# Loading one of six operands in runs of four tokens: a chunked delta-rule attention with a spectral mixer behind it

## The chip, the cores and the metric

The kernel runs on one core of one Trainium2 chip. The metric is the device time of one execution in microseconds (us), where lower is better. Five executions of the kernel before took 219.13 to 220.66 us, with a median of 219.2 us.

## The reference, cut to what matters

Two stages stand behind each other. The first is a recurrence over 768 tokens for each of 4 x 8 = 32 heads with a 40 x 40 state; the second mixes tokens and channels.

```
for t in range(768):                       # state: [B, H, 40, 40]
    y[t]  = r[t] @ state
    Sa    = state @ a[t]
    state = state * w[t] - outer(Sa, b[t]) + outer(v[t], k[t])
x = y as [B, 768, 320]                     # heads side by side
theta = x @ w_theta
y = w_tok_r @ (x * cos(theta)) + w_tok_i @ (x * sin(theta))    # over tokens
u = x + y
out = u + relu(u @ w_ch)
```

All six inputs r, k, v, w, a, b lie in memory as [batch 4, head 8, token 768, 40] in float32. One token of one head is therefore a run of 160 bytes, and the tokens of one head follow each other without a gap.

## The kernel before, in words

The 768 tokens of a batch are cut into 6 chunks of 128, so there are 24 **tiles** (`i` = 0 to 23), each with 128 tokens on the partitions and 8 heads x 40 on the free axis.

`load(i)` gives six transfers a tile, one for each operand (`raw_w`, `raw_kb` twice, `raw_a`, `raw_rv` twice), each read as `"h t d -> t h d"`: 1024 runs of 160 bytes. They are issued from SP's queue (line L414), into four buffers for each operand.

`prep(i)` takes the logarithm of w on ScalarE (ACT) (`ln`, L423), sums it over tokens with triangular matrices on TensorE (PE) (`cs`, L430 to L440), and exponentiates the sums (`exp`, L445) into `ex`, where the two halves hold the inverse and the plain decay. k, b (`kb`, L452) and a (`ah`, L456) are multiplied by them on GpSimd (POOL); r and v are only cast to bf16 on POOL (`rv`, L461). For the first two tiles this is on VectorE (DVE) and ACT instead. Then `transpose_pairs` (L396) turns each bf16 operand on PE, two heads at a time (heads 2g and 2g+1, each padded from 40 to 64, make one 128-wide block), and ACT copies the result out of PSUM (L399), read as 32-bit words: `kbT`, `rvT` (both 1024 bf16 columns, or 512 words) and `aT` (512 columns, or 256 words).

`attention_scores(i)` and `readout(i)` multiply such transposed blocks with each other (L484, two heads side by side in the PE array) and DVE masks the result (L489): `psi`, `phi`, `lamv`, `lamu`, one DVE pass of 128 x 1024 each. `recurrence(i)` carries the state from chunk to chunk (`x0`, `nx`, `nu`, `gt`, `gd`), and the readout gives `x` (L624), which is transposed and multiplied by `w_theta` (L631, first use).

Of each batch, when all six chunks are done, ACT takes sines and cosines (L655), POOL multiplies them with x (`zr`, `zi`, L667), and `mix_row` runs 12 matmuls of 320 columns for each of six output rows (L685), then the residual (L695), a transpose (L588), the channel product (L631), the ReLU and sum (L704) and the store (SP, L707). The token weights for this are fetched once, in six pairs of transfers issued from POOL (`wtok_block`, L725: 128 x 768 of `w_tok_r` and of `w_tok_i`), and transposed on PE (L733). `mixer_weights` fetches `w_theta` and `w_ch` from POOL (L713, L716).

The order of the work is not that of the source. Every step is an `Op` with an assumed cost, the tiles it reads and writes, and a priority from the tables `TIMES` (a due time for each tile, each mixer row and each weight transfer) and `OFF` (an offset for each kind of step). `Plan.order` makes one list from these before anything is issued, and each engine's instructions stand in the order of that list. PSUM has eight banks: four are used as two double banks (`ps_d`, for the scores and `cs`), four as single banks (`ps_s`, for everything else).

Of the kernel before, what the change touches and what calls it, by code (L numbers as in the profile page):

```python
# [9 lines left out]
FP32 = mybir.dt.float32  # L10
# [216 lines left out]
def tail(n):  # L227
# [4 lines left out]
    ah=-29.76, ch=42.32, cs=-23.68, ea=-5.68, egd=-64.18, egt=9.05, ekb=-1.05, enu=-33.25,  # L232
    enut=-26.71, erv=-11.79, eth=-30.49, eut=-42.87, ewt=25.44, ex=-7.68, exp=-112.65,
    ext=9.87, gd=25.41, gt=10.89, kb=6.58, ln=-1.17, load=-12.1, mlu=70.45, mlv=15.71,
    mphi=35.75, mpsi=75.19, nu=-16.23, nut=3.78, nx=-57.27, oo=43, row=42.66, rv=9.85,
    sin=53.93, slu=-3.56, slv=6.28, sphi=-11.65, spsi=-15.12, st=42.29, ta=1.92, th=30.73,
    tkb=-0.04, trv=-1.76, uadd=20.68, ut=30.15, wdma=56, wt=28.14, x0=-37.84, xt=23.63,
    y=-16.87, z=-2.05)
WAIT, TSWITCH = 416.01, 546374.0
TIMES = dict(  # L240
    tile=[
        -39.53, -34.24, -29.51, -3.78, 20.04, 41.89, 38.94, 51.03, 56.49, 58.19, 71.7, 90.01,
        94.38, 97.37, 114.43, 121.89, 126.37, 125.37, 126.65, 137.15, 152.75, 154.06, 155.36,
        173.39],
    row=[
        51.82, 57.24, 68.97, 70.44, 94.9, 101.27, 93.77, 118.11, 124.13, 107.33, 127.65,
        140.22, 116.14, 132.99, 161.62, 121.8, 167.43, 194.51, 178.51, 189.99, 186.39, 240.98,
        241.1, 195.27],
    rel=[
        -29.38, 28.51, 59.76, 33.74, 24.97, 97.39, 29.98, 104.9])  # L250
# [3 lines left out]
def kernel(  # L254
# [35 lines left out]
    raw_rv = sb("raw_rv", [128, 2, H, D], FP32, 4)  # L290

    def load(i):
        bi, ci = divmod(i, NCH)

        def src(ap):
            return ap[bi, :, ci * C:(ci + 1) * C, :].rearrange("h t d -> t h d")
        s = i % 4
        return ((("raw_w", s), raw_w[s], src(w)),
                (("raw_k", s), raw_kb[s][:, 0], src(k)),
                (("raw_b", s), raw_kb[s][:, 1], src(b)),  # L300
                (("raw_a", s), raw_a[s], src(a)),
                (("raw_r", s), raw_rv[s][:, 0], src(r)),
                (("raw_v", s), raw_rv[s][:, 1], src(v)))
# [34 lines left out]
    rv_t = padded("rv", [128, 2, H, 64], NRV, last24)  # L338
# [12 lines left out]
    ex_t = sb("ex", [128, 2, 328], FP32, NEX)  # L351
    aT_t = sb("aT", [128, 512], BF16, NTR)
    kbT_t = sb("kbT", [128, 1024], BF16, NTR)
    rvT_t = sb("rvT", [128, 1024], BF16, NTR + 1)
# [57 lines left out]
    def loads(i):  # L412
        for key, dst, src in load(i):
            add("SP", "load", i, lambda dst=dst, src=src: nc.sync.dma_start(out=dst, in_=src),  # L414
                650, [], [key], work=1030)

    def prep(i):
# [3 lines left out]
        kb, rv, ah = kb_t[i % NKB], rv_t[i % NRV], ah_t[i % 3]  # L421
        kex = ("ex", i % NEX)
        add("ACT", "ln", i, lambda: nc.scalar.activation(  # L423
            out=lw[:, :, 0:D], in_=raw_w[s4], func=AF.Ln), 473,
# [3 lines left out]
        def cs():  # L428
            t = ps(pk)
            nc.tensor.matmul(t[:, 0, 0:DM], lhsT=ntri_inc, rhs=lw[:, :, 0:D],  # L430
# [6 lines left out]
            for g in range(G):  # L437
                nc.tensor.matmul(t[:, 1, DM + 2 * g:DM + 2 * g + 2], lhsT=pair(lw, g),
                                 rhs=ones2, start=False, stop=True, skip_group_check=True)
            nc.tensor.matmul(t[:, 0, DM:DM + 8], lhsT=ident,  # L440
                             rhs=off_diag.rearrange("p g c -> p (g c)"),
                             start=True, stop=True, skip_group_check=True)
        add("PE", "cs", i, cs, 2 * mm(320) + 6 * 25, [("lw", s2)], [pk], new=(pk, 2),
            tail=tail(8))
        add("ACT", "exp", i, lambda: nc.scalar.activation(  # L445
            out=ex, in_=ps(pk)[:, :, 0:328], func=AF.Exp), 717, [pk], [kex], table="lnexp")
        invW = ex[:, 0, 0:DM].rearrange("p (h d) -> p h d", h=H)
        Wi = ex[:, 1, 0:DM].rearrange("p (h d) -> p h d", h=H)
        fast = i < 2
        for j, nm in enumerate("kb"):  # L450
            add("DVE" if fast else "POOL", "kb", i,
                lambda j=j: (nc.vector if fast else nc.gpsimd).tensor_tensor(  # L452
                    out=kb[:, j, :, 0:D], in0=raw_kb[s4][:, j], in1=invW, op=ALU.mult),
                490 if fast else 864, [("raw_" + nm, s4), kex], [("kb", j, i % NKB)])
        add("DVE" if fast else "POOL", "ah", i,
            lambda: (nc.vector if fast else nc.gpsimd).tensor_tensor(  # L456
                out=ah[:, :, 0:D], in0=raw_a[s4], in1=Wi, op=ALU.mult),
            490 if fast else 864, [("raw_a", s4), kex], [("ah", i % 3)])
        for j, nm in enumerate("rv"):
            add("ACT" if fast else "POOL", "rv", i,  # L460
                lambda j=j: (nc.scalar.copy if fast else nc.gpsimd.tensor_copy)(  # L461
                    out=rv[:, j, :, 0:D], in_=raw_rv[s4][:, j]),
                460, [("raw_" + nm, s4)], [("rv", j, i % NRV)])

        def tr(kind, kinde, srcs, dst, skeys, dkey, eng):
# [8 lines left out]
        tr("trv", "erv", (rv[:, 0], rv[:, 1]), rvT_t[i % (NTR + 1)],  # L474
           [("rv", 0, i % NRV), ("rv", 1, i % NRV)], ("rvT", i % (NTR + 1)), "ACT")
# [18 lines left out]
    def attention_scores(i):  # L494
        st, s2 = i % NTR, i % NSC
        kbT, aT, rvT = kbT_t[st], aT_t[st], rvT_t[i % (NTR + 1)]
# [4 lines left out]
        scores(i, "slv", "mlv", rvT[:, 512:], rvT[:, 0:512], [("rvT", i % (NTR + 1))],  # L501
               lamv_t[s2], ("lamv", s2), mask_p)

    def recurrence(i):
        first, last = i % NCH == 0, i % NCH == NCH - 1
        st, s2 = i % NTR, i % 2
        aT, kb, rv = aT_t[st], kb_t[i % NKB], rv_t[i % NRV]
# [3 lines left out]
        vb = rv[:, 1]  # L511
        pk = ("ps", "x0", i)

        def x0():
# [13 lines left out]
            [("aT", st), ("psi", i % NSC), ("rv", 1, i % NRV)] +  # L528
# [14 lines left out]
        if not last:  # L543
            gk = ("ps", "gt", i)

            def gt_mm():
# [12 lines left out]
                [("kb", 0, i % NKB), ("kb", 1, i % NKB), ("rv", 1, i % NRV), ("nu", s2)] +  # L559
# [254 lines left out]
```

## Time and profile before

| | |
|---|---|
| median of five runs | 219.2 us |
| the profiled execution's own time | 219.2 us |
| its span, first to last instruction | 217.3 us |
| TensorE clock granted | 0.999 |
| PE busy | 196.8 us (91%), 3368 matmuls |
| DVE busy | 165.9 us (76%) |
| ACT busy | 146.7 us (68%) |
| POOL busy | 118.4 us (54%) |
| loads and stores of SP's queue (q1) | 153216 packets, 27.54 MB, 70.1% of the 16 DMA engines' span |
| weights of POOL's queue (q0) | 2432 packets, 2.77 MB, 7.7% |

An engine's busy time is the union of its instructions' times, and matmuls that overlap in the array count once, so a PE that is busy all the time need not be at its peak. "Packets" are the pieces that the DMA engines move, one for each contiguous run. The page also cuts the span into 40 equal slices and gives the busy share of each in tenths.

### The profile page before, as it was taken

To read this page: it belongs to the slowest core of one execution; us is meant where nothing else is said; L and a number is where in the kernel's file an instruction comes from. 1 tells how busy PE (TensorE), PEld (TensorE's weight loads), DVE (VectorE), ACT (ScalarE), POOL (GpSimd) and SP (SyncE) were. 2 spreads that over 40 slices of the span, in tenths; PEclk is the share of its full clock that TensorE was granted. 3 is DMA by queue.
4 is the path that set the end of the run, shared out by engine and by line. 5 is a ranking of instruction groups with operands and counts; after the bars stand their busy time and mean duration, and the time that the engine had idled before them with its cause. 6 is when DMAs were issued, how large, how long until landed. Compare 5 with 4: busy or idle time off the path is not lost.

```text
span 217.3 us, 8118 instructions
## 1 busy us (share of the span) xinstructions
PE 196.8 (91%) x3368; PEld 155.5 (72%) x3368; DVE 165.9 (76%) x250; ACT 146.7 (68%) x319; POOL 118.4 (54%) x184
## 2 busy tenths in 40 slices
PE   1497898879897899999999999999999999999993
PEld 1375766657677688687787778878787888777771
DVE  7468678875989758888999668888979978866533
ACT  3356675978679769978459946899599764863111
POOL 5000688297673992894762972697658660165000
PEclk9999999999999999999999999999999999999999
DMA  6998999999999999999988999898897010101122
GB/s 112 195 186 152 168 154 161 177 178 160 159 184 165 172 182 160 181 199 182 170 151 160 150 188 156 179 182 153 151 209 128 33 63 5 60 33 60 33 91 91
DMA packets 155684, 30.81 MB, mean 142 GB/s; under 512 B 150400, under 2 KB 155648, under 8 KB 155648
## 3 DMA queue, kind: packets, MB, share of 16 engines
q1 hardware_dynamic: 153216, 27.54, 70.1%
q0 software_dynamic: 2432, 2.77, 7.7%
q8 instruction: 26, 0.43, 0.8%
q14 instruction: 10, 0.08, 0.1%
HBM read 29.13 MB, written 3.93 MB: 152 GB/s over the span
## 4 chain that ended last, share of the span: by engine, by line
PE 72%; DVE 9%; ACT 5%; DMA 5%; POOL 3%; issue 3%; SPq 1%; ACTq 0%; DVEq 0%; POOLq 0%
PE ps_s L685 19%; PE ps_s L396 14%; PE ps_d L484 10%; PE ps_s L631 8%; PE ps_s L588 4%; DVE lamu L489 3%; DMA wrow_i<-in_moe_w_tok_i_dram 3%; DMA raw_a<-in_a_dram 2%; PE ps_s L617 2%; PE ps_s L536 2%; DVE psi L489 2%; PE ps_s L524 2%; PE ps_s L554 2%; PE ps_s L615 2%; DVE phi L489 2%
## 5 line engine op out<-in xcount | busy, mean ns | idle before, releaser
L452 POOL TENSOR_TENSOR kb<-raw_kb,ex 128x320 bf16<-128x320 f32 x44 | 37.4, 862 | 18.1 <-ACT ex L445 16.5
L685 PE MATMUL ps_s<-zr,wtok_r 128*128 128x320 bf16 x144 | 40.9, 300 | 0.2 <-ACT gd L572 0.2
L685 PE MATMUL ps_s<-zi,wtok_i 128*128 128x320 bf16 x144 | 40.8, 299 | 0.0
L489 DVE TENSOR_TENSOR psi<-ps_d,mask_p 128x1024 bf16<-128x1024 f32 x24 | 29.3, 1221 | 9.3 <-PE ps_d L484 9.2
L456 POOL TENSOR_TENSOR ah<-raw_a,ex 128x320 bf16<-128x320 f32 x22 | 19.0, 862 | 28.0 <-ACT ex L445 22.8
L489 DVE TENSOR_TENSOR lamv<-ps_d,mask_p 128x1024 bf16<-128x1024 f32 x24 | 29.1, 1219 | 6.2 <-PE ps_d L484 6.1
L667 POOL TENSOR_TENSOR zr<-cs,x 128x320 bf16<-128x320 f32 x23 | 17.8, 792 | 28.6 <-ACT cs L655 28.6
L489 DVE TENSOR_TENSOR lamu<-ps_d,mask_p 128x1024 bf16<-128x1024 f32 x24 | 29.0, 1219 | 4.6 <-PE ps_d L484 4.3
L489 DVE TENSOR_TENSOR phi<-ps_d,mask_n 128x1024 bf16<-128x1024 f32 x24 | 29.1, 1216 | 0.8 <-PE ps_d L484 0.7
L445 ACT ACTIVATE ex<-ps_d 128x656 f32<-128x656 f32 x24 | 17.2, 719 | 7.5 <-PE ps_d L440 6.4
L461 POOL CAST rv<-raw_rv 128x320 bf16<-128x320 f32 x44 | 18.6, 449 | 0.0
L399 ACT COPY kbT<-ps_s 128x512 f32<-128x512 f32 x24 | 14.1, 587 | 6.1 <-PE ps_s L396 5.7
L484 PE MATMUL ps_d<-aT,kbT 64*128 64x128 bf16 x384 | 16.8, 221 | 1.5 <-ACT ex L445 0.7
L695 DVE TENSOR_TENSOR u<-ps_s,x 128x320 bf16<-128x320 f32 x24 | 11.7, 488 | 8.1 <-PE ps_s L685 7.9
L667 POOL TENSOR_TENSOR zi<-cs,x 128x320 bf16<-128x320 f32 x23 | 17.8, 791 | 0.0
L399 ACT COPY uT<-ps_s 128x192 f32<-128x192 f32 x24 | 7.5, 320 | 14.8 <-PE ps_s L588 14.8
L685 PEld LDWEIGHTS <-wtok_r 128*128 128x128 bf16 x144 | 14.0, 98 | 4.6
L396 PE MATMUL ps_s<-ident,kb 128*128 128x128 bf16 x192 | 15.7, 223 | 1.7 <-DVE kb L452 1.3
L685 PEld LDWEIGHTS <-wtok_i 128*128 128x128 bf16 x144 | 14.1, 98 | 4.1 <-issue 0.4
L624 DVE TENSOR_TENSOR x<-ps_s,ex 128x320 bf16<-128x320 f32 x24 | 11.7, 487 | 6.5 <-PE ps_s L617 5.7
L617 PE MATMUL ps_s<-kb,lamu 128*128 128x40 bf16 x192 | 15.0, 180 | 1.3 <-DVE lamu L489 1.2
L399 ACT COPY rvT<-ps_s 128x512 f32<-128x512 f32 x24 | 14.2, 593 | 2.9 <-PE ps_s L396 2.7
(109 smaller groups left out, 546.5 us busy)
## 6 DMA issues: line engine op xcount, KB each, us to landing
raw_w<-in_w_dram SPq DMA_DIRECT2D x24, 160.0 KB, 3.8
raw_kb<-in_k_dram SPq DMA_DIRECT2D x24, 160.0 KB, 3.8
raw_kb<-in_b_dram SPq DMA_DIRECT2D x24, 160.0 KB, 3.8
raw_a<-in_a_dram SPq DMA_DIRECT2D x24, 160.0 KB, 4.6
raw_rv<-in_r_dram SPq DMA_DIRECT2D x24, 160.0 KB, 4.4
raw_rv<-in_v_dram SPq DMA_DIRECT2D x24, 160.0 KB, 4.3
out_dram<-oo SPq DMA_DIRECT2D x24, 160.0 KB, 1.8
wrow_r<-in_moe_w_tok_r_dram POOLq DMA_DIRECT2D x6, 192.0 KB, 4.8
```

The source lines that it names most:

```text
L396: nc.tensor.transpose(out=dst[:, c:c + 128], in_=pair(src, g), identity=ident)
L399: nc.scalar.copy(out=out.bitcast(FP32), in_=in_)
L445: add("ACT", "exp", i, lambda: nc.scalar.activation(out=ex, in_=ps(pk)[:, :, 0:328], func=AF.Exp), 717, [pk], [kex], table="lnexp")
L452: lambda j=j: (nc.vector if fast else nc.gpsimd).tensor_tensor(out=kb[:, j, :, 0:D], in0=raw_kb[s4][:, j], in1=invW, op=ALU.mult),
L456: lambda: (nc.vector if fast else nc.gpsimd).tensor_tensor(out=ah[:, :, 0:D], in0=raw_a[s4], in1=Wi, op=ALU.mult),
L461: lambda j=j: (nc.scalar.copy if fast else nc.gpsimd.tensor_copy)(out=rv[:, j, :, 0:D], in_=raw_rv[s4][:, j]),
L484: nc.tensor.matmul(t[:, q, g, :], lhsT=lhs[rows(q), g * 128:(g + 1) * 128], rhs=rhs[rows(q), g * 128:(g + 1) * 128], start=True, stop=True)
L489: add("DVE", kindm, i, lambda: nc.vector.tensor_tensor(out=dst.rearrange("p a b c -> p (a b) c"), in0=ps(p).rearrange("p a (g c) -> p (a g ...
L617: nc.tensor.matmul(o, lhsT=lamu[:, p, g, :], rhs=kb[:, 1, h, 0:D], start=False, stop=True, skip_group_check=True)
L631: nc.tensor.matmul(dst, lhsT=lhs[:, kt, :], rhs=rhs[:, kt, :], start=kt == 0, stop=kt == 2)
L667: nc.vector if fast else nc.gpsimd).tensor_tensor(
L685: nc.tensor.matmul(ps(pk)[:, 0:DM], lhsT=wtok[nm][:, s, j * 128:(j + 1) * 128], rhs=zs[c][:, s], start=n == 0 and c == 0, stop=n == NT - 1 ...
```

## The change

The r operand is loaded differently, and what follows from that is adapted.

- `raw_rv` becomes `raw_v` and `raw_r`. Of r, 128 tokens of four heads (a half `c` of the eight heads, `g` = 0 to 3 in it) are one transfer: the partition is (t, g) with t = 0 to 31 a group of four tokens, and on the free axis lie the four tokens q x 40, which is one run of 640 bytes in memory. Two such transfers make a tile, so a tile has seven loads.
- POOL casts r in one instruction as before; the four tokens q are then four 128-wide blocks (half 0 and half 1 of the heads, padded to 64). PE transposes the four blocks into a bank of its own (`tr`), and ACT copies them out (`er`) with a reordering read, from columns (q, t, g) to (g, t, q), 2-byte elements one by one. v has its own transpose (`tv`) and its own copy (`ev`, 256 words).
- One block now holds heads g and g+4, not 2g and 2g+1. w, k, b, a, v are therefore written in that order when they are first touched (`natural` to `paired`), and `x` is put back in the order of the heads by the readout's product with `ex`.
- In `cs` the first of the two sums is written to the end of its bank, so that both sums and the mask columns are one contiguous stretch of 648 columns; one matmul of 8 columns a tile is gone, and `exp` reads 648 columns in place of 656.
- `OFF`, `TIMES` and two weights of the planner have other values, so the order of the steps is another on every engine.

```diff
-    raw_rv = sb("raw_rv", [128, 2, H, D], FP32, 4)
+    raw_v = sb("raw_v", [128, H, D], FP32, 4)
+    raw_r = sb("raw_r", [128, 2, 4 * D], FP32, 4)
...
-                (("raw_r", s), raw_rv[s][:, 0], src(r)),
-                (("raw_v", s), raw_rv[s][:, 1], src(v)))
+        rr = r[bi, :, ci * C:(ci + 1) * C, :].rearrange("(c g) (t q) d -> c t g (q d)", c=2, q=4)
...
+                [("raw_v", s), raw_v[s], src(v)],
+                *([("raw_r", s, c), raw_r[s][:, c], rr[c]] for c in range(2)))
...
-    rv_t = padded("rv", [128, 2, H, 64], NRV, last24)
+    v_t = padded("v", [128, H, 64], NRV, last24)
+    r_t = padded("r", [128, 4, 2, 64], 2, last24)
...
-    rvT_t = sb("rvT", [128, 1024], BF16, NTR + 1)
+    rT_t = sb("rT", [128, 512], BF16, NTR + 1)
+    vT_t = sb("vT", [128, 512], BF16, NTR)
...
+    def natural(t):
+        return t.rearrange("p (c g) d -> p g c d", c=2)
+    def paired(t):
+        return t.rearrange("p (g c) d -> p g c d", c=2)
...
-            out=lw[:, :, 0:D], in_=raw_w[s4], func=AF.Ln), 473,
+            out=paired(lw)[:, :, :, 0:D], in_=natural(raw_w[s4]), func=AF.Ln), 473,
...
-            nc.tensor.matmul(t[:, 0, 0:DM], lhsT=ntri_inc, rhs=lw[:, :, 0:D],
+            nc.tensor.matmul(t[:, 0, 512 - DM:512], lhsT=ntri_inc, rhs=lw[:, :, 0:D],
...
-            nc.tensor.matmul(t[:, 0, DM:DM + 8], lhsT=ident,
-                             rhs=off_diag.rearrange("p g c -> p (g c)"),
-                             start=True, stop=True, skip_group_check=True)
...
-            out=ex, in_=ps(pk)[:, :, 0:328], func=AF.Exp), 717, [pk], [kex], table="lnexp")
+            out=ex, in_=ps(pk).rearrange("p a b -> p (a b)")[:, 512 - DM:512 + DM + 8],
+            func=AF.Exp), 710, [pk], [kex], table="lnexp")
...
-                    out=kb[:, j, :, 0:D], in0=raw_kb[s4][:, j], in1=invW, op=ALU.mult),
+                    out=paired(kb[:, j])[:, :, :, 0:D], in0=natural(raw_kb[s4][:, j]), in1=invW, op=ALU.mult),
...
-        for j, nm in enumerate("rv"):
-            add("ACT" if fast else "POOL", "rv", i,
...
+        add("ACT" if fast else "POOL", "v", i,
+            lambda: copy(out=paired(vb)[:, :, :, 0:D], in_=natural(raw_v[s4])),
+            460, [("raw_v", s4)], [("v", i % NRV)])
+        add("ACT" if fast else "POOL", "r", i,
+            lambda: copy(out=rb[:, :, :, 0:D],
+                         in_=raw_r[s4].rearrange("p c (q d) -> p q c d", q=4)),
+            460, [("raw_r", s4, 0), ("raw_r", s4, 1)], [("r", i % 2)])
...
-        tr("trv", "erv", (rv[:, 0], rv[:, 1]), rvT_t[i % (NTR + 1)],
-           [("rv", 0, i % NRV), ("rv", 1, i % NRV)], ("rvT", i % (NTR + 1)), "ACT")
+        tr("tv", "ev", (vb,), vT_t[i % NTR], [("v", i % NRV)], ("vT", i % NTR), "ACT")
...
+            for q in range(4):
+                nc.tensor.transpose(out=t[:, q * 128:q * 128 + 128],
+                                    in_=rb[:, q].rearrange("p c d -> p (c d)"), identity=ident)
+        add("PE", "tr", i, tr_r, 4 * mm(128), [("r", i % 2)], [pr], new=(pr, 1), tail=tail(128))
+        rT = rT_t[i % (NTR + 1)]
+        add("ACT", "er", i, lambda: nc.scalar.copy(
+            out=rT.rearrange("p (g t q) -> p g t q", g=G, q=4),
+            in_=ps(pr).bitcast(BF16)[:, 0:512].rearrange("p (q t g) -> p g t q", q=4, g=G)),
+            592, [pr], [("rT", i % (NTR + 1))])
...
-            out=x[:, 0:DM], in0=ps(pk)[:, 0:DM], in1=ex_t[i % NEX][:, 1, 0:DM],
+            out=x[:, 0:DM].rearrange("p (c g d) -> p g c d", c=2, g=G),
+            in0=ps(pk)[:, 0:DM].rearrange("p (g c d) -> p g c d", c=2, g=G),
+            in1=ex_t[i % NEX][:, DM:2 * DM].rearrange("p (g c d) -> p g c d", c=2, g=G),
...
```

## The prediction

> **What bounds the kernel now.** I read the slices of the span first, then busy times by stage, then the waits of POOL and ACT, then the rows of the instructions that the change touches.
>
> ```profile
> span 217.3 us, 8118 instructions
> ...
> PE   1497898879897899999999999999999999999993
> ...
> DMA  6998999999999999999988999898897010101122
> ...
> q1 hardware_dynamic: 153216, 27.54, 70.1%
> q0 software_dynamic: 2432, 2.77, 7.7%
> ```
>
> The PE row has holes until slice 15 (about 80 us) and is full after that. The DMA row is full from slice 3 to slice 31 (about 168 us). So two resources take turns: first the loads feed PE too slowly, then PE has a backlog. The same in numbers (columns: stretch, its length, busy of PE, PEld, DVE, ACT, POOL with instruction counts, PE clock, DMA share, GB/s):
>
> ```profile
> 0.00:10.00 10.00, 3.31 (x36) 2.52 (x36) 5.49 (x46) 4.22 (x7) 3.39 (x14) 1.00 0.92 153
> 10.00:20.00 10.00, 8.03 (x123) 5.89 (x119) 7.30 (x10) 5.67 (x14) 0.00 (x0) 1.00 0.97 161
> 20.00:80.00 60.00, 51.96 (x1004) 41.43 (x1006) 46.44 (x53) 44.32 (x96) 41.42 (x63) 1.00 1.01 170
> 80.00:167.00 87.00, 86.70 (x1567) 69.79 (x1567) 73.11 (x91) 68.62 (x149) 57.77 (x86) 1.00 0.96 171
> 167.00:214.00 47.00, 46.85 (x647) 35.91 (x645) 33.10 (x53) 23.90 (x56) 15.81 (x23) 1.00 0.14 47
> ```
>
> PE idles 6.69 + 1.97 + 8.04 = 16.7 us before 80 us and 0.30 + 0.15 = 0.45 us from 80 to 214. A microsecond saved on DMA after 80 us is therefore worth nothing by itself, and the end can move only by as much as the PE work moves forward out of the first 80 us, or by less PE work. No other engine is full in 20 to 80: DVE is busy 77%, ACT 74%.
>
> ```profile
> POOL ah L456 <- ACT ex L445: 19.0, 2, 16.8
> ...
> ACT aT L399 <- PE ps_s L396: 4.2, 5, 2.2
> ...
> SPq L414 <- POOL rv L461: 5.1, 6, 1.7
> ```
>
> These are waits between 10 and 80 us (total, times, longest). Engines wait for each other's newest tile; SP waits for a raw buffer only a few microseconds, while the DMA engines are never empty. That is a feed-limited stage.
>
> **What the Trainium skill says.** "DMA: Bandwidth & Descriptors", section Specifications, puts the smallest run for full rate at 512 bytes. The trace agrees that 160 bytes are dear (below). Its rules for kernel authors say that transfers from several queues share the same 16 engines; the trace agrees, since SP's loads take 3.8 us to land in the median and raw_a at 68.3 us takes 6.9 us with two weight transfers beside it. "PSUM — Partial Sum Buffer", Specifications, gives cachelines of 8 bytes and says that non-contiguous patterns slow matmuls; of ACT it says nothing, and no instruction of this trace reads PSUM in 2-byte elements far apart.
>
> **Part 1, the r transfers.** From q1: 0.701 x 217.3 us x 16 / 153216 = 15.9 ns of one engine for a packet, nearly all of 160 bytes. An r tile is 1024 packets: 1024 x 15.9 / 16 = 1.02 us of all engines. For 640 bytes there is no row. Stores are 1280 bytes a run, and this stretch has nothing else:
>
> ```profile
> 200.00:210.00 10.00, 10.00 (x83) 7.31 (x82) 5.09 (x11) 1.75 (x6) 0.00 (x0) 1.00 0.20 67
> ```
>
> 0.20 x 16 x 10 us over 670 KB / 1280 = 523 packets is 61 ns. Between the two, in a straight line, 640 bytes cost 35 ns, and the new r tile 256 x 35 / 16 = 0.56 us. Saving 0.46 us a tile, 10.9 us in all; the bounds are 61 ns (saving 0.04 us a tile) and 15.9 ns (0.76 us). q1 should fall to 153216 - 24 x 768 + 24 x 16 = 135168 packets (the last term: one more completion packet on each engine and tile). Only the tiles up to 80 us count, ten of them: 4.6 us. SP issues seven transfers, not six; an issue takes 0.53 us at least in the rows of raw_rv, so 3.9 us a tile against a feed of some 6: nothing, as long as the feed is slower than that. SP takes them in order, so an r transfer that waits for POOL's cast holds back the loads behind it, as rv's cast does now (5.1 us above).
>
> **Part 2, the order.** The instruction order shows that POOL issued its first three pairs of weights before tile 9's products are cast, and now issues none before them. A pair is two of twelve such transfers, which make 2.30 of q0's 2.77 MB: 0.077 x 217.3 x 2.30 / 2.77 / 12 = 1.16 us each, so three pairs are 7.0 us of DMA that tiles 5 to 9 no longer stand behind. What is late next: the mixer rows of batch 0, at PE's matmul 1188 against 1098, and the tiles from 10 on, which share DMA with six pairs (14 us); PE has the rows of batch 0 to fill that.
>
> Parts 1 and 2 give up to 4.6 + 7.0 = 11.6 us of earlier data for tile 9. PE can use at most its 8.04 idle us of 20 to 80 and what its busy count hides (1004 matmuls in 60 us there, 1567 in 87 us after). DVE, at 46.4 us busy in that stage, would be at 87% in 53 us. I take 7 us of gain; bounds 2 and 11.
>
> **Part 3, PE.** One matmul of 8 columns a tile less. In the timeline the next starts about 25 ns after it, so 24 x 0.025 = 0.6 us. tv and tr are the same eight transposes. Gain 0.6 us (0.3 if only those after 80 us count).
>
> **Part 4, ACT.**
>
> ```profile
> L399 ACT COPY rvT<-ps_s 128x512 f32<-128x512 f32 x24 | 14.2, 593 | 2.9 <-PE ps_s L396 2.7
> ...
> L399 ACT COPY aT<-ps_s 128x256 f32<-128x256 f32 x24 | 9.1, 377 | 7.4 <-PE ps_s L396 7.2
> L445 ACT ACTIVATE ex<-ps_d 128x656 f32<-128x656 f32 x24 | 17.2, 719 | 7.5 <-PE ps_d L440 6.4 <-issue 0.8
> ```
>
> One copy of 512 words (593 ns) becomes one of 256 words like aT (377 ns) and `er` of 512 elements. "ScalarE: Activation LUTs", What ACT_TABLE_LOAD costs, prices an ACTIVATE at 186 + 0.833 ns an element whatever its type, an estimate of 612 ns; the 593 of the 512-element row is used. So 24 x 377 = 9.0 us more, less 24 x 8 x 0.833 = 0.2 us in `ex`. The cover is ACT's idle time, 15.7 us of 20 to 80 and 18.4 us of 80 to 167, which lose 3.8 and 5 us. Behind `er` queue the copies that the recurrence waits for (`nx`, `nu`), and slv waits for `er` itself; one more single bank of four is taken a tile. I charge 1.0 us (0 to 3). If `er` is slower than 593 the cover goes; see the rival.
>
> **Part 5, at nothing.** The POOL products and casts, `ln` and the DVE product into `x` have the same element counts in another order of 40-element runs; POOL has 18.6 of 60 us idle to cover a rise (at 10% of 862 ns, 24 x 3 x 0.09 = 6 us). The start is the same: the first four loads are w, k, b, a in both.
>
> **Sum.** -7.0 - 0.6 + 1.0 = -6.6 us. The profiled execution took 219.2 us, 1.9 us more than its span, and the median of the runs is 219.2 too: 212.6, so 212.5 us.
>
> **Rivals.**
> - *The whole feed counts.* All 10.9 us of part 1 and the order's gain reach the end, capped by PE's 16.7 us idle less the 8.7 us of the first 20 us: some 8 to 11 us and the 0.6, with ACT hidden: 208 us. For it: PE is full after 80 us, so whatever is moved ahead comes off the end. Against it: DVE and ACT are three quarters busy already in that stage.
> - *Hidden.* The feed is faster but DVE and ACT, with waits on both sides, keep the tile's pace, and 9 us of added ACT work eat the rest: 219 us. Signs: DMA holes before 80 us with PE still short.
> - *ACT becomes the bound (slower).* `er` reads 2-byte elements 256 bytes apart. If it takes twice 593 ns, ACT gets 9.0 + 14.2 = 23 us more; in 80 to 167 it would be busy 68.6 + 14 x 0.97 = 82 of 87 us, with the recurrence's copies in the same queue. That undoes 6.6 us and adds 4: 223 us. The tipping point is about 0.9 us for `er`. For it: two slices of ACT are at 9 already. Against it: no ACT row of this trace is slower than its element count.
> - *The runs are not one packet.* Then q1 stays near 153216 and the DMA time as it is; the order alone gives 216 us. It is part of the first case's range.
>
> **How the numbers follow.** Likeliest case 0.54 (209.5 to 217), whole feed 0.14, hidden 0.13, ACT bound 0.19. A change within 0.5%, 1.1 us, can't be told from none here. Faster 0.54 + 0.14 = 0.68, same 0.13, slower 0.19. The range 207.5 to 220.5 leaves out most of the ACT case and the low end of the second.
>
> **What would show it.** Right: q1 at 135168 packets and about 141 us of DMA (now 0.701 x 217.3 = 152), tile 9's last load landing some 8 us before 68.5 us, PE full from about 72 us on, `er` near 593 ns. Wrong: `er` above 0.9 us or ACT waits of 10 us before DVE and PE; PE idle before 80 us still over 14 us; or new PE idle after 80 us, above all in the stretch where the six pairs load.

## The result, and the profile after

The changed kernel takes 0.9944 of the time of the kernel before, with a 95% interval of 0.9921 to 0.9966: 1.2 us less (0.7 to 1.7), where 6.6 us were forecast. The ratio counts only executions within 1.5% of the fastest of their own kernel, which are 77 of 80 for the kernel before but 14 of 43 for the kernel after (most of the other 29 with a granted clock of 0.996 or more, too); over all of them the medians are 219.68 us before and 219.84 us after, and the means 219.9 and 220.1 us. So a gain is not shown for a typical execution of the kernel after, and where a later run is compared with it, both the ratio and the means over all executions are given. The profiled execution below took 220.48 us, close to that mean.

First the slices and the queues of the kernel after:

```profile
span 218.7 us, 8116 instructions
...
PE   1588899879999898999998899999999999999993
...
DMA  6998989899889969989699999879989500002122
...
q1 hardware_dynamic: 135168, 27.54, 66.6%
q0 software_dynamic: 2432, 2.77, 8.5%
```

Two things differ from before. The DMA row now has five eights and two sixes in slices 6 to 20, where it had nines, while PE is still short of 9 in some of the slices up to 16: the transfers have become cheaper and PE has not become full. And PE has eights in slices 22 and 23 (about 115 to 126 us), where it had none. The stages of the kernel after (columns as in the prediction):

```profile
0.00:10.00 10.00, 2.91 (x29) 2.20 (x31) 5.18 (x47) 3.78 (x6) 3.39 (x14) 1.00 0.90 154
10.00:20.00 10.00, 9.27 (x126) 7.19 (x121) 6.64 (x9) 5.91 (x15) 0.00 (x0) 1.00 0.90 163
20.00:80.00 60.00, 53.71 (x1066) 42.98 (x1065) 49.80 (x55) 50.48 (x115) 42.16 (x63) 1.00 0.92 160
80.00:167.00 87.00, 84.13 (x1479) 67.72 (x1479) 69.50 (x91) 65.00 (x149) 54.80 (x82) 1.00 0.93 170
167.00:214.00 47.00, 46.95 (x650) 35.85 (x648) 32.83 (x51) 26.61 (x59) 18.57 (x26) 1.00 0.22 58
80.00:140.00 60.00, 57.20 (x988) 45.53 (x987) 47.51 (x62) 47.21 (x103) 37.98 (x57) 1.00 0.95 167
```

In 20 to 80 us PE does 1066 matmuls where it did 1004. So work did move forward, but PE's idle time there fell only from 8.0 to 6.3 us. In 80 to 167 us it does 1479 where it did 1567, and idles 2.9 us where it idled 0.3, nearly all of it before 140 us. The lead is spent again. What PE waits for there is told by PE's waits of the kernel after in 80 to 167 us (total, times, longest):

```profile
PE ps_d L443 <- ACT lw L436: 1.3, 2, 1.0
PE ps_s L400 <- POOL v L472: 1.0, 1, 1.0
PE ps_s L494 <- POOL r L475: 0.4, 1, 0.4
```

These three are the first steps behind the loads of w, v and r. The chain of the kernel after in the same stretch (start, length, what) goes through the transfers themselves:

```profile
78.72 5.20 DMA raw_w<-in_w_dram
84.00 0.48 ACT lw L436
...
111.16 4.97 DMA raw_v<-in_v_dram
116.25 0.46 POOL v L472
...
120.38 4.75 DMA raw_w<-in_w_dram
125.22 0.48 ACT lw L436
```

So the loads are late after 80 us, in the stretch into which the weight pairs were moved: the six pairs have landed at 73.9, 84.2, 93.5, 100.9, 128.7 and 134.5 us, where in the kernel before they have at 42.8 to 112.9 us. Last, ACT's rows of the kernel after:

```profile
L455 ACT ACTIVATE ex<-ps_d 128x648 f32<-128x648 f32 x24 | 17.2, 715 | 6.1 <-PE ps_d L451 4.6 <-DVE psi L515 1.1 <-issue 0.2
L498 ACT COPY rT<-ps_s 128x512 bf16<-128x512 bf16 x24 | 14.0, 588 | 3.3 <-PE ps_s L494 3.1
...
L403 ACT COPY vT<-ps_s 128x256 f32<-128x256 f32 x24 | 9.2, 383 | 3.3 <-PE ps_s L400 3.3
```

The reordering copy takes 588 ns for 512 elements, as the one of 512 words did (593).

### The profile page after: what moved, and what is told of

Same layout as the page of the kernel before. It is cut to its first block, busy times and chain, and to the rows that moved or that the text cites. A ratio compares the mean times of both kernels' runs of the same rounds, so it can differ in the third digit from the quotient of the medians.

```text
span 218.7 us, 8116 instructions
## 1 busy us (share of the span) xinstructions
PE 198.3 (91%) x3344; PEld 156.5 (72%) x3344; DVE 165.4 (76%) x252; ACT 152.1 (70%) x343; POOL 118.9 (54%) x184
## 3 DMA queue, kind: packets, MB, share of 16 engines
q1 hardware_dynamic: 135168, 27.54, 66.6%
## 4 chain that ended last, share of the span: by engine, by line
PE 67%; DMA 11%; DVE 9%; ACT 8%; issue 3%; SPq 1%; POOL 0%; ACTq 0%; DVEq 0%; POOLq 0%
PE ps_s L712 17%; PE ps_s L400 11%; PE ps_d L510 9%; PE ps_s L658 7%; DMA raw_w<-in_w_dram 7%; PE ps_s L613 3%; DMA raw_a<-in_a_dram 2%; DVE psi L515 2%; PE ps_s L642 2%; DMA raw_v<-in_v_dram 2%; PE ps_s L549 2%; PE ps_s L760 2%; PE ps_s L640 2%; DVE lamv L515 2%; DVE phi L515 2%
## 5 line engine op out<-in xcount | busy, mean ns | idle before, releaser
L467 POOL TENSOR_TENSOR ah<-raw_a,ex 128x320 bf16<-128x320 f32 x22 | 19.0, 863 | 40.3 <-ACT ex L455 39.8
L712 PE MATMUL ps_s<-zr,wtok_r 128*128 128x320 bf16 x144 | 40.4, 299 | 0.1
L455 ACT ACTIVATE ex<-ps_d 128x648 f32<-128x648 f32 x24 | 17.2, 715 | 6.1 <-PE ps_d L451 4.6
L510 PE MATMUL ps_d<-aT,kbT 64*128 64x128 bf16 x384 | 17.7, 223 | 2.0 <-DVE lamu L515 0.8
L498 ACT COPY rT<-ps_s 128x512 bf16<-128x512 bf16 x24 | 14.0, 588 | 3.3 <-PE ps_s L494 3.1
L510 PEld LDWEIGHTS <-kbT 64*128 64x128 bf16 x384 | 11.7, 96 | 6.3 <-issue 3.0
L403 ACT COPY uT<-ps_s 128x192 f32<-128x192 f32 x24 | 7.6, 324 | 12.2 <-PE ps_s L613 12.1
L555 ACT CAST nx<-ps_s 128x320 bf16<-128x320 f32 x24 | 10.2, 426 | 8.2 <-PE ps_s L549 8.0
```

The costliest lines, as they stand in the source:

```text
L403: nc.scalar.copy(out=out.bitcast(FP32), in_=in_)
L455: add("ACT", "exp", i, lambda: nc.scalar.activation(out=ex, in_=ps(pk).rearrange("p a b -> p (a b)")[:, 512 - DM:512 + DM + 8], func=AF.Ex ...
L467: lambda: (nc.vector if fast else nc.gpsimd).tensor_tensor(out=paired(ah)[:, :, :, 0:D], in0=natural(raw_a[s4]), in1=Wi, op=ALU.mult),
L498: add("ACT", "er", i, lambda: nc.scalar.copy(out=rT.rearrange("p (g t q) -> p g t q", g=G, q=4), in_=ps(pr).bitcast(BF16)[:, 0:512].rearra ...
L510: nc.tensor.matmul(t[:, q, g, :], lhsT=lhs[rows(q), g * 128:(g + 1) * 128], rhs=rhs[rows(q), g * 128:(g + 1) * 128], start=True, stop=True)
L712: nc.tensor.matmul(ps(pk)[:, 0:DM], lhsT=wtok[nm][:, s, j * 128:(j + 1) * 128], rhs=zs[c][:, s], start=n == 0 and c == 0, stop=n == NT - 1 ...
```

## The experiments

All ratios are to the kernel before, with the 95% interval. "Kernel after" and "kernel before" name what each edit starts from. They ask in turn whether layout or order matters, whether the feed limits, what the late weights and ACT's added work cost, and what does hold PE back before 80 us.

### Layout and order apart

The first run is the changed kernel with the planner's tables of the kernel before; the second is the kernel before with the planner's tables of the changed one. Steps that only one of them has take the value of their counterpart, as shown.

```diff
-WAIT, TSWITCH = 478.73, 929209.0
+    er=-11.79, ev=-11.79, tr=-1.76, tv=-1.76, r=9.85, v=9.85, loadr=-12.1,
...
+WAIT, TSWITCH = 416.01, 546374.0
```

> The new layout of r with the order constants of the kernel before (each new step takes the constants of the old one that it comes from). Theory A, the layout relieves DMA but the compute engines keep the tile's pace, and the weights moved behind tile 9 then collide with the loads: the old order, with early weights, keeps the layout's small gain, about 217 to 219 us. Theory B, the layout is a loss by itself (9 us more ACT work) and only the new order makes up for it: 222 us or more. Theory C, the new order is what costs and the layout brings the 6 us that were forecast: 213 us.

Measured: 225.39 us, ratio 1.0261 (1.0214 to 1.0309).

```diff
-WAIT, TSWITCH = 416.01, 546374.0
+    erv=-8.3, trv=1.62,
...
+WAIT, TSWITCH = 478.73, 929209.0
```

> The old layout of r with the order constants of the changed kernel. Theory A: DMA is short where the weights arrive late, and r costs more of it: 222 us or more. Theory B: the order brings what the layout loses: 216 us or less. Theory C: the order costs some 5 us: 224 us.

Measured: 239.72 us, ratio 1.0903 (1.0853 to 1.0952), 15 us beyond the largest number that any of the theories named. Neither half stands alone: the new layout under the old tables loses 2.6%, and the old layout under the new tables 9.0%. The forecast's sum, which took the two as separate gains, has no counterpart in these runs. What the layout costs by itself they don't tell, as tables that go with one list of steps can be poor for another.

### Is the stage before 80 us limited by the feed?

**No loads at all.** The kernel before, without the loads of tiles 4 to 23 and without all but two of the weight pairs; the old contents of the buffers are used again, every other instruction stays. Then the same for the kernel after.

```diff
-            add("SP", "load", i, lambda dst=dst, src=src: nc.sync.dma_start(out=dst, in_=src),
+            add("SP", "load", i, (lambda: None) if i >= 4 else lambda ...
...
-            add("POOL", "wdma", 2 + tb, lambda row=row, ap=ap: nc.gpsimd.dma_start(
+            add("POOL", "wdma", 2 + tb, (lambda: None) if tb >= 2 else lambda ...
```

> The same for the kernel before: its order, no loads after tile 3, two of six weight pairs. The forecast's first step says that its first 80 us are short of data; then 209 us or less, and PE has issued clearly more by 80 us. If the order and the engines are the pace there too: 215 to 218 us.

Measured: ratio 1.0000 (0.9978 to 1.0022). The stages of the kernel before without loads:

```profile
20.00:80.00 60.00, 52.03 (x987) 41.84 (x988) 46.73 (x53) 43.36 (x94) 38.70 (x58) 0.97 0.22 36
80.00:167.00 87.00, 86.70 (x1561) 69.70 (x1558) 71.96 (x91) 68.66 (x148) 54.96 (x81) 1.00 0.06 19
```

The DMA share falls from 1.01 to 0.22, and PE's busy time stays at 52.0 of 60 us (for 987 matmuls where there were 1004, at a granted clock of 0.97 in this stage). The idle 8 us of PE are there with no feed to wait for. More of this run's executions had a lower granted clock than of the kernel before beside it; at like clocks it is faster by 0.7 us (218.6 against 219.2, at 0.996 or more, 5 and 17 executions) and by 0.3 us (220.1 against 220.4, below that, 17 and 13). So the loads cost at most a fraction of a microsecond, where the first step needed 7. **That is the verdict on the forecast's first step.**

> The changed kernel, same order, with no loads after tile 3 and two of six weight pairs: every engine's work as before, DMA nearly empty. What is left is the pace of the engines in this order. Theory A: little less than without r alone, 213 to 215.5 us, and the same work issued by 80 us. If loads still set the pace before 80 us: 208 us or less.

Measured: ratio 0.9866 (0.9831 to 0.9901). Stages of the kernel after without loads:

```profile
20.00:80.00 60.00, 53.50 (x1063) 42.91 (x1061) 49.49 (x54) 50.67 (x114) 42.14 (x63) 1.00 0.17 28
80.00:140.00 60.00, 59.68 (x1052) 48.27 (x1050) 50.55 (x67) 47.59 (x104) 36.71 (x54) 1.00 0.09 23
```

Before 80 us nothing changes here either (53.50 against 53.71). From 80 to 140 us PE gets back 2.5 us. With hardly any transfers the new layout and order are worth 1.3%, 2.9 us; the transfers take 0.8% of it back by the ratio, and all of it by the means (217.2 us here against 220.1).

**The transfers of r alone.** The kernel before and its order; r comes in two transfers of 640-byte runs, its values in other places than the sums expect.

```diff
+        rr = r[bi, :, ci * C:(ci + 1) * C, :].rearrange("(c g) (t q) d -> c t g (q d)", c=2, q=4)
...
+            for c in range(2):
+                nc.sync.dma_start(out=flat[:, 160 * c:160 * c + 160], in_=rr[c])
```

> The kernel before with its own order; only r comes in two transfers of 640-byte runs a tile instead of one of 160-byte runs. The values of r so land in other places, which the sums don't undo. Relay theory: the DMA engines' time falls by about 0.6 us a tile, and the whole by nothing, ratio 0.998 to 1.002. Forecast's theory (the feed sets the pace before 80 us): 9 tiles by 0.6 us or more come off, ratio 0.97 to 0.98. A rival: SP issues seven transfers a tile instead of six, 0.65 us each, and falls behind: ratio 1.00 to 1.02.

Measured: ratio 0.9986 (0.9966 to 1.0006). The part of the change that gives it its name is worth 0.3 us, and nothing within the interval. Tile 9's last load lands at 68.6 us there, at 68.5 us before: SP issues a load when its buffer comes free, so cheaper packets only leave the DMA engines empty for longer.

**No loads of r** beyond tile 3, in the kernel after.

```diff
+                (lambda: None) if small and i >= 4 else
                 lambda dst=dst, src=src: nc.sync.dma_start(out=dst, in_=src),
```

> The changed kernel, same order, but r is transferred for the first four tiles only (later tiles compute with stale r). This takes 40 of 48 r transfers, some 14 us of DMA work, away, which is more than the change saved. Theory A: before 80 us nothing is gained, and only the collisions of 80 to 167 us get shorter: 2 to 3 us less than the changed kernel. If DMA still sets the pace: 8 us less or more.

Measured: ratio 0.9854 (0.9813 to 0.9896). Tile 9's v now lands at 57.4 us instead of 65.8, more than the forecast's 8 us sooner. PE starts on that tile's `ah` at 66.6 us instead of 67.4. Data that come 8 us early are used 0.8 us early. What this run gains, it gains later: PE is busy 59.70 us of 80 to 140, where the kernel after has 57.20.

The two profiled kernels say the same of this tile. In the kernel before its a lands at 67.1 us, and POOL takes it up at 74.1, behind a weight issue and five products for the mixer; in the kernel after it lands at 64.0, and POOL takes it up at 66.1. PE's work on `ah` of this tile moves from 75.6 to 67.4 us, 8.2 us, with data that come 3.1 us sooner: POOL's order did most of it.

**The loads by themselves.** Nothing but transfers: after one large store, 24 whole loads from 9.4 us, then 24 pairs of half loads in 640-byte runs from 40.3 us; then a stretch of both kinds, in which most whole loads wait for their buffers.

> Nothing but transfers (the output is zeros): 24 loads of 160 KB in runs of 160 bytes, then 24 pairs of 80 KB in runs of 640 bytes, then eight tiles of five loads and one pair as in the changed kernel. The forecast's price was 0.56 us a pair against 1.02 us a load. If the runs themselves are as cheap as that, the second stretch takes 24 x 0.56 = 13 us and the first 24. If the 640-byte packets are dearer (the changed kernel's queue share says 0.70): 17 us.

Measured, stretches of that kernel (length, DVE and POOL busy, clock, DMA share, GB/s):

```profile
9.40:40.30 30.90, 0.00 (x0) 0.00 (x0) 1.00 1.18 242
40.30:71.70 31.40, 0.00 (x0) 0.00 (x0) 1.00 0.59 132
```

The first stretch also holds the store, and is not used further. In the second the DMA engines are 59% busy and 24 pairs take 31.3 us, 1.31 us a pair: SP's issue of 0.65 us for each transfer is the limit, not the packets, and neither of the expected times came. (In the last stretch a pair takes SP 1.24 us as well, with the DMA engines still emptier.) The mean of a packet in the trace of the kernel after is 15.1 ns for 160 bytes, 43.7 ns for the 640 of r (half of them take 32 or less) and 59 ns for the 1280 of the stores, so an r tile takes 256 x 43.7 / 16 = 0.70 us of all engines instead of 1024 x 15.1 / 16 = 0.97.

### What the late weights cost

**Four of the six weight pairs left out**, in the kernel after (the old rows are transposed again).

```diff
-            add("POOL", "wdma", 2 + tb, lambda row=row, ap=ap: nc.gpsimd.dma_start(
+            add("POOL", "wdma", 2 + tb, (lambda: None) if tb >= 2 else lambda ...
```

> The changed kernel, same order, but four of the six pairs of token weights are not transferred (their rows are transposed from stale buffers). This takes 9 us of DMA work out of the stretch from 80 to 140 us. Theory A: the PE idle time that is new there goes, 2 to 3 us less than the changed kernel. If the loss has nothing to do with the late weights: no difference beyond 1 us.

Measured: ratio 0.9883 (0.9834 to 0.9932), and in its stages:

```profile
20.00:80.00 60.00, 53.74 (x1066) 43.02 (x1064) 49.79 (x55) 50.64 (x115) 42.12 (x63) 1.00 0.92 162
80.00:140.00 60.00, 59.69 (x1052) 48.24 (x1050) 50.55 (x67) 47.72 (x104) 36.64 (x53) 1.00 0.78 146
```

PE's holes of 80 to 140 us are gone (59.69 against 57.20 busy) and the time is lower by about as much as without any loads. The intervals of this run and of the kernel after overlap a little; the stages are the clearer reading. And all 17 executions of the three runs that take transfers from the kernel after (no r, no loads, these pairs) took 216.0 to 218.7 us, where its own take 216.1 to 223.6. So after 80 us the transfers do limit, by 0.3 us for each pair left out by the ratios and 0.7 us by the means (217.3 us against 220.1).

**The pairs issued earlier**, in the kernel after, with six buffers instead of two.

```diff
-    wrow = dict(r=sb("wrow_r", [128, S], BF16, 2), i=sb("wrow_i", [128, S], BF16, 2))
+    wrow = dict(r=sb("wrow_r", [128, S], BF16, 6), i=sb("wrow_i", [128, S], BF16, 6))
...
+    for tb, tile_n in enumerate((3, 5, 6, 8, 10, 12)):
+        at = next(n for n, o in enumerate(order) if o.kind == "ah" and o.i == tile_n)
+        order[at + 1:at + 1] = pairs[tb]
```

> The changed kernel with six buffers a name for the rows of the six late weight pairs instead of two, and these pairs issued by POOL right behind the ah of tiles 3, 5, 6, 8, 10 and 12; every other order is that of the changed kernel. Theory (a relay between engines sets the pace before 80 us, and the late weight pairs delay loads between 80 and 140 us): the gain of leaving the pairs out, or most of it, about 1.0 to 1.3 us below the changed kernel, ratio to the kernel before 0.987 to 0.990, PE 59 us or more of 80 to 140 us. Rival (the DMA engines bound the stretch before 80 us): the pairs are back in the feed's way and most of 7 us is lost, ratio 1.01 to 1.03. A third: the pairs cost POOL's and the queue's time wherever they stand, ratio 0.994 as before.

Measured: 224.91 us, ratio 1.0224 (1.0178 to 1.0271): a clear miss of the relay theory's expectation, 0.987 to 0.990. Four pairs have landed by 66.5 us, where the kernel before has three by 75 and the kernel after one by 74. Tile 9's v lands at 70.6 us instead of 65.8, and the first mixer row starts at 85.2 us instead of 78.2. The stage and the chain of this kernel:

```profile
20.00:80.00 60.00, 48.68 (x948) 38.13 (x949) 44.03 (x47) 45.33 (x102) 40.84 (x63) 1.00 0.97 168
```

```profile
60.83 2.75 DMA raw_r<-in_r_dram
...
63.71 0.46 POOL r L475
64.17 0.65 SPq L420
...
71.07 0.59 SPq L420
71.66 0.04 issue
71.70 4.79 DMA raw_a<-in_a_dram
76.50 0.07 issue
76.56 0.84 POOL ah L467
```

This is what a feed-limited stage looks like: from 54 to 77 us the chain is SP's queue, transfers, and the POOL products that wait for them, and no PE or DVE piece. The feed has no slack to lose, then, and yet nothing to gain: adding three pairs (7.0 us of DMA, by the forecast's price of 1.16 us for each of the six transfers) costs PE 7.0 us at the first mixer row, and taking everything away gives it nothing. That the two numbers are alike proves nothing, though: issuing three pairs takes POOL 3.4 us as well, in front of its products, and on tile 9's `ah` PE is 3.8 us later. No run tells POOL's time and the transfers' apart.

### ACT's added work

**A short `er`**, in the kernel after: 128 of the 512 elements are copied, and its 24 copies take 6.4 us instead of 14.0.

```diff
-            out=rT.rearrange("p (g t q) -> p g t q", g=G, q=4),
...
+            out=rT.rearrange("p (g t q) -> p g t q", g=G, q=4)[:, 0:1],
...
```

> The changed kernel, same order, but ACT copies only a quarter of the transposed r (128 of 512 elements; the rest of rT stays zero). ACT gets 24 x 0.3 = 7 us less work, so that it stands near the kernel before. Theory A1, the copies on ACT set the pace before 80 us: 3 us less than the changed kernel or more, and the work that PE has issued by 80 us rises. Theory A2, no single engine is it, the fixed order and the latencies between engines are: under 1.5 us.

Measured: ratio 0.9918 (0.9884 to 0.9953), which overlaps the kernel after's; the mean of its nine executions is 218.6 us, 1.5 us below the kernel after's. **The same copies in the kernel before**, its order and transfers unchanged: the copy of `rvT` is cut in two, and r's columns come in another order.

```diff
...
+                    copy_words(dst[:, 512:1024], ps(p)[:, 256:512])
+                    nc.scalar.copy(
+                        out=dst[:, 0:512].rearrange("p (g t q) -> p g t q", g=G, q=4),
+                        in_=ps(p).bitcast(BF16)[:, 0:512].rearrange("p (q t g) -> p g t q", q=4, g=G))
```

> The kernel before with its own order; only ACT's copy of the transposed r and v is cut in two, 256 words of v and 512 reordered elements of r, so that r's columns come in another order than the sums expect. ACT gains about 0.35 us a tile, 8 to 9 us in all. Theory (ACT's extra work lies in its gaps): ratio 1.000 to 1.005. Rival (ACT's extra work takes from 80 us on what the transfers gave): half of it or more shows, 4 us or more, ratio 1.018 to 1.04.

Measured: 222.35 us, ratio 1.0109 (1.0064 to 1.0154), between the two expectations. The two copies take 23.8 us in the rows where the one took 14.2. These 9.6 us cost 2.4 us in the order of before; in the order of the kernel after, taking 7.6 off gives 0.6 us by the ratios, which is within the intervals, and 1.5 us by the means, with an uncertainty of 1.0. "ACT has 15.7 us idle" does not make such work free. That it depends on who stands behind it in the order is the likely reason, and not shown.

### What holds PE back before 80 us

The view that answers this is PE's own waits, which the forecast did not use. For the kernel before, 20 to 80 us:

```profile
PE ps_d L484 <- DVE phi L489: 1.1, 1, 1.1
PE ps_s L396 <- ACT nu L540: 1.0, 2, 0.7
PE ps_d L484 <- ACT ex L445: 0.7, 2, 0.4
PE ps_d L484 <- DVE psi L489: 0.7, 2, 0.3
PE ps_s L396 <- POOL ah L456: 0.5, 1, 0.5
...
PE ps_s L733 <- DMA wrow_i<-in_moe_w_tok_i_dram: 0.2, 1, 0.2
```

Fifteen rows of small waits, the longest 1.1 us, in all 7.4 of the 8.0 us of idle time: twelve are for results of DVE or ACT, the masks and the recurrence above all, two for POOL's products behind the loads, and one, of 0.2 us, for a transfer. Six runs ask whether one of the suppliers stands for all.

**No sines for the first half of batch 0**, kernel before (`z` holds 0.3 instead, filled by POOL at the start).

```diff
...
+        if o.i == 2 and o.kind in ("sin", "z"):
+            continue
```

> The kernel before with its own order, its sines and the two products z of the first half of batch 0 left out with the table loads that they need; z holds 0.3 instead. All transfers stay. Relay theory (ACT's sines at 37 to 44 us, then POOL's z, then ah, kb, rv, then DVE's masks hold PE's feeding engines at 40 to 62 us): ACT loses about 5 us and POOL about 4 us on the chain, and the whole 3 to 6 us, ratio 0.973 to 0.986, with PE's idle time of 20 to 80 us down by as much. Forecast's theory (the DMA engines set the pace there): 0 to 1 us, ratio 0.995 to 1.000. A rival (the time comes back behind 80 us, where PE is full): PE idle before 80 falls, ratio near 1.000 only if PE's total is then what is left: 0.99.

Measured: ratio 0.9918 (0.9884 to 0.9952), 1.8 us, less than the relay theory asked for. The next three halve one engine's work each, in the kernel before; the halves left out are filled once, by POOL, at the start.

```diff
-            out=dst.rearrange("p a b c -> p (a b) c"),
...
+            out=dst[:, 0],
...
```

> The kernel before with its own order and all its transfers; DVE masks one half only of each of psi, phi, lamv and lamu (512 of 1024 elements, the other half is zero), so each of its 96 mask instructions falls from 1.22 to about 0.65 us, some 55 us of DVE in all and 22 us of them in 20 to 80 us. Theory DVE (the row of masks in the chain of waits sets the pace there): PE's idle 8 us of 20 to 80 us falls to 3 us or less, ratio 0.970 to 0.985. Theory of ties (several suppliers are late by about as much, so one of them alone gives little): 1 to 3 us, ratio 0.986 to 0.995. Feed: ratio 0.998 to 1.002.

Measured: 0.9876 (0.9805 to 0.9948).

```diff
-            add(eng, kind, i, lambda: copy_words(dst, ps(psk)[:, 0:n // 2]),
+            add(eng, kind, i, lambda: copy_words(dst[:, 0:n // 2], ps(psk)[:, 0:n // 4])
+                if kind in ("ekb", "erv", "ea", "enut") else copy_words(dst, ps(psk)[:, 0:n // 2]),
...
```

> The kernel before with its own order and all its transfers; ACT copies one half only of kbT, rvT, aT and nuT (the other halves are zero), about 0.21, 0.21, 0.1 and 0.1 us less in each tile, some 15 us of ACT in all. Theory ACT (its copies set the pace before 80 us): 4 us or more come off, ratio below 0.982. Theory of ties: 0.5 to 2.5 us, ratio 0.989 to 0.998. Feed: 0.998 to 1.002.

Measured: 0.9929 (0.9902 to 0.9955).

```diff
-                    out=kb[:, j, :, 0:D], in0=raw_kb[s4][:, j], in1=invW, op=ALU.mult),
+                    out=kb[:, j, 0:4, 0:D], in0=raw_kb[s4][:, j, 0:4], in1=invW[:, 0:4], op=ALU.mult),
...
```

> The kernel before with its own order and all its transfers; POOL (and DVE and ACT for tiles 0 and 1) makes kb, ah and rv for heads 0 to 3 only, the others are zero: about 0.43 us less in each of 66 products, 0.2 us in each of 44 copies, some 37 us of POOL in all. Theory POOL: 4 us or more come off, ratio below 0.982. Theory of ties: 0.5 to 2.5 us, ratio 0.989 to 0.998. Feed: 0.998 to 1.002.

Measured: 0.9919 (0.9879 to 0.9959). Then the three together:

> The three edits together, DVE's masks, ACT's copies and POOL's products halved, the kernel before's order and all its transfers. Theory of ties: more comes off than with any alone, 5 us or more, ratio 0.965 to 0.977, and what PE still waits for before 80 us is then the transfers. Theory of one engine: no more than its own run gives. Feed: ratio 0.998 to 1.002. If the pace is PE's own order of instructions, with nothing late, ratio 0.995 to 1.000 too, but then PE's idle time before 80 us stays without any releaser.

Measured: 0.9938 (0.9916 to 0.9959), which as a time says little: POOL's fills at the start took 11 us there, and PE's first transposes of `ah` began at 12.1 us. But in the other four these transposes began at 7.0 to 7.3 us, where the kernel before has 8.1. The fills had moved something: POOL issues the first two weight transfers behind them, the first at 5.8 to 7.3 us instead of 2.8, and tile 0's a landed at 6.4 or 6.5 us instead of 7.5. Hence a control: the kernel before with such a fill and nothing else.

```diff
+    nc.gpsimd.memset(zr_t[0], 0.0)
+    nc.gpsimd.memset(zi_t[0], 0.0)
```

> The kernel before, with nothing changed but that POOL fills two of its z buffers with zeros at its start (they are written again later), some 3.3 us, and so issues the first two weight transfers 3.3 us later. It is the control for the runs in which POOL filled halves at its start: there tile 0's a landed at 6.4 us instead of 7.6 and its transposes began 1.1 us sooner. If that came from the later weights: 0.8 to 1.4 us faster, ratio 0.993 to 0.997, and the gains of leaving out the first sines, of half the ACT copies and of half the POOL products are within 1 us of nothing. If it came from those edits: ratio 0.999 to 1.001.

Measured: 218.41 us, ratio 0.9951 (0.9931 to 0.9972). In all seven traces with a fill tile 0's a lands at 6.3 to 6.5 us; in eleven of the twelve without, where the weights are issued at 2.8 us, it lands at 7.3 to 8.0, and in that of the six buffers at 6.3. So the delay is common, but not in every execution. 40 to 70% of what the four runs gained is this start.

Against the control the first sines, half the ACT copies and half the POOL products are worth 0.2 to 0.3%, half the masks 0.75% (1.6 us for 51 us of DVE), and all four intervals overlap the control's: **no single supplier holds the 8 us.**

Measured in the profiles from PE's first `ah` to the start of the last mixer row, the control takes 202.0 us, half masks 199.8, half copies 201.2, half products 202.5 (with the granted clock at 0.94 in 50 to 80 us), and all three together 197.0: 5.0 us less, where the three apart sum to 2.5. That speaks for many suppliers that are each about equally late, but it is one profile of each, and the run with all three starts 4.9 us later than the control, with the loads of its first tiles under way all the same: some of the 5.0 us can be that. In the run with all three, the chain of 20 to 80 us goes through a weight transfer, and so does that of the kernel before; first the one, then the other:

```profile
68.65 0.49 POOL wrow_r L734
69.21 6.05 DMA wrow_i<-in_moe_w_tok_i_dram
75.31 0.51 PE ps_s L742 x6
```

```profile
69.07 5.66 DMA wrow_i<-in_moe_w_tok_i_dram
74.78 0.51 PE ps_s L733 x6
```

PE's fixed order wants the row at 75 us. It waits for it 0.2 us in the kernel before, the last row of PE's waits above, and 0.5 us in the run with all three. So the transfer is one more of those that are about equally late. Which of the many waits comes first in which tile is not settled by these runs.

### A version that beats both

The kernel after, with the control's fill and nothing else.

> The changed kernel with the same fill by POOL at its start and nothing else. If the first weights stand in the way of tile 0's a: tile 0's transposes begin near 7.4 us instead of 8.5, 0.8 to 1.4 us less than the changed kernel, ratio to the kernel before 0.988 to 0.991, which beats both. If the changed kernel gives the start back later, in the loads that collide from 80 us on: ratio 0.993 to 0.995.

Measured: 217.03 us, ratio 0.9864 (0.9832 to 0.9895), a little more than was expected and below the kernel after's interval; the mean of all six executions, one of 221.2 us among them, is 217.6 us, 2.4 us below the kernel after's with an uncertainty of 1.6. Tile 0's first transposes begin at 7.0 us instead of 8.5, and the lead is kept: the last mixer row starts at 208.9 us instead of 211.6. Its stages:

```profile
20.00:80.00 60.00, 54.31 (x1078) 43.24 (x1078) 48.63 (x53) 50.66 (x114) 42.77 (x64) 1.00 0.93 164
80.00:140.00 60.00, 57.92 (x1023) 46.80 (x1018) 49.39 (x65) 46.96 (x101) 39.53 (x60) 1.00 0.98 172
```

The holes of 80 to 140 us are still 2.1 us deep. PE starts 1.4 us sooner, and idles 0.6 us less in 20 to 80 us and 0.7 us less in 80 to 140 than in the trace of the kernel after. A fill of 3.3 us on POOL is a crude way to hold back two transfers, and it gains more than the change did.

## Why the prediction was wrong, point by point

- **The bound, the step that failed: "first the loads feed PE too slowly ... That is a feed-limited stage."** The DMA row was full and PE had holes, and the one was taken for the cause of the other. Without loads the holes stay at 8.0 us and the ratio is 1.000. A DMA row is full here because SP issues as early as buffers come free; it tells nothing on whether anyone waits. The waits quoted for it were those of POOL, ACT and SP, and 16.8 of the 19.0 us of POOL's row are one wait before its first product. PE's own, above, name DVE and ACT for most of the idle time: small waits in a fixed order of steps, none of which stands for all.
- **Part 1, the price.** 135168 packets came out exactly, so the runs are one packet each, and the fourth rival fell. The 35 ns for 640 bytes, drawn between two rows, are 43.7 ns in the trace, so a tile saves 0.27 us of DMA and not 0.46, and q1 takes 0.666 x 218.7 = 145.6 us, not 141. "DMA: Bandwidth & Descriptors" of the Trainium skill, section Specifications, puts full rate at 512 bytes; in this trace 640 bytes in 43.7 ns are 14.6 bytes a ns and 1280 bytes in 59 ns are 21.7, and by the medians, 32 and 55 ns, 20.0 and 23.3. The packet's rate still rises above 512 bytes, then, but the one are loads and the other stores, and they ran beside other transfers. The size of the term doesn't matter, though: alone it is worth 0.3 us of time. SP's seven issues are 7 x 0.53 = 3.7 us, not 3.9, and with the 0.65 us of the run of loads alone 4.6, still under the 6 us of a tile.
- **Part 2, the order.** The three pairs did move, but tile 9's last load landed at 66.4 us, 2 us early and not 8, and PE's gain on that tile came mostly from POOL's order. "PE has the rows of batch 0 to fill that" failed as well: PE idles 2.9 us in 80 to 167 us, and four pairs left out undo it. The forecast named this stretch as the place where it could go wrong, and its other sign came too: PE idles 14.1 us before 80 us, just over the 14 that it named.
- **Part 3, PE.** The 24 matmuls are gone (3368 to 3344). Their 0.6 us were not measured apart.
- **Part 4, ACT.** `er` takes 588 ns where 593 were taken, and "ScalarE: Activation LUTs", What ACT_TABLE_LOAD costs, comes to an estimate of 612. The charge of 1.0 us (0 to 3) holds: shortening it gives 0.6 us by the ratios and 1.5 by the means. That the cover was ACT's idle total is not what makes it hold, as the 2.4 us in the kernel before show.
- **The rivals.** *Hidden*, at 0.13, came nearest: its sign, DMA holes before 80 us with PE still short, is what the slices show, and its 219 us are close to the mean of all executions. Of its reason the half on DVE and ACT before 80 us fits PE's waits; but the rest is eaten by the late transfers of 80 to 140 us more than by ACT's added work. *Whole feed* fell with the first step, and *ACT bound* with `er` at 588 ns.
- **Where the 1.2 us come from.** With hardly any transfers the new order and layout gain 1.3%, some 2.9 us, from the order and the lost matmuls, which no run tells apart. The transfers after 80 us take 1.7 us of it back by the ratio, and all of it by the means. The result lies inside the range, but the value hung on one reading: without the 7.0 us of the first step the same sum gives +0.4 us.

## What to carry to other kernels

A full DMA row beside a hungry PE is a coincidence until PE's own waits name the loads, or until a run without the loads is faster; ask those two first, and count a feed's speed-up as nothing until they say otherwise. A resource can have nothing to gain and nothing to lose at once: test it in both directions before moving load from one stage into another. An experiment that fills buffers at its start needs a control with the fill alone, and here the control was the better optimization.

## What was not expected of the hardware

- SP's issue took about 0.65 us for a transfer of 80 KB, so 24 pairs of half loads by themselves took 31.3 us with the DMA engines 59% busy.
- ACT read 512 2-byte PSUM elements, in groups of four that lie 256 bytes apart, in 588 ns in the kernel after and in 606 ns in the kernel before with these copies, about as fast as 512 words in a row (593 ns).
- Two weight transfers, the first issued 2.8 us after the start, go with a tile 0's a that lands 1.1 us later in most traces; held back by 3.3 us, the whole gains 0.5% in the kernel before and 0.8% in the kernel after.
